# Attention and MoE block in one kernel: PSUM banks with fixed uses, 0.87 MoE steps a slot up to slot 108, chunk rows taken a slot later and loaded by one transfer

## The chip, the core and the metric

The kernel runs on one core of one Trainium2 chip. The core has a matrix engine (TensorE, PE in the profile, with its weight loads as PEld), a vector engine (VectorE, DVE), an activation engine (ScalarE, ACT), GpSimd (POOL) and an engine that here only issues transfers (SyncE, SP). Each works through its own instructions in order and waits for others by semaphores. Matmuls write into PSUM, which has 8 banks of 512 float32 columns in 128 partitions. The metric is the device time of one execution in microseconds (us); of several runs the median counts.

## The reference

Decay attention over 8 batches of 8 heads, 576 positions and head size 64, then a layer norm with a two-layer ReLU network on the 4608 tokens of width 512:

```python
scores = scale * np.matmul(q, k.transpose(0, 1, 3, 2))
cum = np.cumsum(np.log(np.clip(f, 0.0001, 1.0)), axis=-1)
decay = cum[:, :, :, None] - cum[:, :, None, :]
scores = np.where(causal, -1000000000.0, scores + decay)
attn = np.exp(scores - np.max(scores, axis=-1, keepdims=True))
attn = attn / (np.sum(attn, axis=-1, keepdims=True) + 1e-09)
x = np.matmul(attn, v)            # heads side by side: 8 x 576 x 512
...
xn = (x - mu) / np.sqrt(var + 1e-06) * g_ln
ch = np.maximum(xn @ w_ch1, 0.0) @ w_ch2     # 512 -> 2048 -> 512
return x + ch
```

## The kernel before

**Slots.** The attention of the 64 heads is cut into slots (line 1115): a head n has four, t = 1 to 4, one for each 128 rows of scores (the 64 rows of t = 0 go with t = 1). 7 more slots empty the pipeline. The loop of line 1132 goes through the slots u and calls, letter by letter, the pieces of an order string (lines 59 to 63; from slot 56 on the third). So the program order on every engine is written out by hand. The letters that matter here: Q scores of this slot's rows (qk_mm), S their row maxima on VectorE (softmax_a, line 411), e the exponential (ACT), B the normalising (POOL), t the transposition of a slot some slots back (transpose_unit, 2 slots back before head 14 and 4 from there on, when the rows first go through a transfer, move, letter D), h and l the high and low halves of the transposed parts (ACT line 522, VectorE line 527), A the product with v (av_unit, at t = 2 and 4), F and a its way out of PSUM (ACT line 606, VectorE line 617). From slot 56 on A, t and Q are dealt into one sequence (dealt). Matmuls are made of float32 halves, a high and a low one, so most products appear two or three times.

**MoE steps.** Between them runs the network over chunks of 256 tokens. One step is 1/16 of a chunk: M computes 128 hidden units of its tokens (mm1, lines 649 to 651, twelve matmuls into a bank h), r and m take their high and low half (ACT line 657, VectorE line 662), N adds the second layer of the step before into two accumulator banks acc0 and acc1 (mm2, lines 671 to 673, six matmuls). 14 chunks (224 steps) are made in this way, the last 1024 tokens by another scheme at the end, the wide part (wide_part). A slot has a step when can() says that the weights and the tokens are there (line 1153); R (rest) sets the limit of chunks whose attention is done, prefetches the next chunk's x (chunk_load, chunk_split, lines 633 and 634), and with 5 and 3 steps to go transposes the chunk's rows back (chunk_rows, line 694, rows loaded by rows_load two steps earlier, four transfers each). After a chunk's last mm2, chunk_out (line 731) takes the result from acc and stores it, within N.

**After the slots.** What is left of the 224 steps follows in the loop of line 1258, and with each of these steps one of five pieces of preparation for the wide part (wide_start): loads, differences (POOL line 903), splits (ACT line 915).

**PSUM.** Two banks are the accumulators. The other six are one ring: bank(name) gives the next of the six to whatever asks, be it scores (s), transposed parts (tr, tr_4b), products with v (o), hidden units (h) or rows (xp). A bank's next user waits for the readers of its last one.

**Numbers.** The steps before stand in slots 38 to 69, 74 to 105 and 107 to 262, and 4 of them after the slots.

Of the kernel before, what the change touches and what calls it, by code (L numbers as in the profile page):

```python
# [17 lines left out]
P = 128  # L18
KT = DM // P
# [12 lines left out]
LAG, LAG_MOVED = 2, 4  # L32
AV, AV_MOVED = 1, 3
MOVED = 14
PLAIN_CHUNKS = 14
WIDE = (NCHUNK - PLAIN_CHUNKS) // 2
PAIRS = FT // 2
EVEN_FROM = 1000
SUMS_FROM = 92
# [19 lines left out]
ORDERS = [  # L59
    (0, "WwbQsSthAeMrgFmlLNPaRf"),  # L60
    (37, "WwbQSstAMhPelgLNFrfmBRa"),
    (56, "WwAthQFlMSPNgreamLRDBZ"),
]
# [3 lines left out]
def attn_moe(ctx: ExitStack, tc: tile.TileContext, qk, v, f, g, w1, w2, out):  # L67
# [302 lines left out]
    def qk_mm(h, t):  # L370
        q0, m, w = QT[t]
        todo = []

        def mm(*a, **k):
            todo.append(lambda: nc.tensor.matmul(*a, **k))  # L375

        cuts = [(0, w)] if w <= 512 else [(0, w // 2), (w // 2, w)]
        h.s = getattr(h, "s", {})
        h.s[t] = []
        for i, (a, z) in enumerate(cuts):  # L380
            sp = bank(f"s{h.n}_{t}_{i}")[:m, : z - a]
            xq, kl = h.xq[:, q0 : q0 + m], h.kl[:, a:z]
            if h.plain:
                mm(sp, xq, kl, start=True, stop=True)
            else:
                mm(sp, h.hi[:, 0, q0 : q0 + m], h.hi[:, 1, a:z], start=True, stop=False)
                mm(sp, xq, kl, start=False, stop=True)
            h.s[t].append((a, z, sp))
        return todo
# [65 lines left out]
    def transpose_unit(h, t):  # L455
# [11 lines left out]
        if t <= 2:  # L467
            tp = bank(f"tr{n}_{t}")
            if t == 1:
                tr(tp[0:64, 0:128], rows_of(h, 0)[:, 0:D])  # L470
                tr(tp[0:64, 64:192], pt[:, 0:64])
                tr(tp[:, 192:320], pt[:, 64:192])
            else:
                tr(tp[0:64, 0:128], pt[:, 0:64])
                tr(tp[:, 128:256], pt[:, 64:192])
                tr(tp[:, 256:384], pt[:, 192:320])
            h.banks = [tp]
        else:
            tp = bank(f"tr{n}_{t}").rearrange("p (k c) -> p k c", k=4)
            tr(tp[0:64, 0, :], pt[:, 0:64])  # L480
            for k in range(1, 4):
                tr(tp[:, k, :], pt[:, 64 + P * (k - 1) : 64 + P * k])
            h.banks = [tp]
            if t == 4:
                tp = bank(f"tr{n}_4b")[:, :P]
                tr(tp, pt[:, 64 + 3 * P : 64 + 4 * P])
                h.banks.append(tp)
# [41 lines left out]
    def av_unit(h, t):  # L529
        po = bank(f"o{h.n}_{t}")  # L530
        todo = []
# [111 lines left out]
    def mm1(c):  # L643
        j = c.j
        c.j += 1
        fs = slice(P * j, P * j + P)
        ph = bank(f"h{c.n}_{j}")[:, :C]
        for k in range(KT):
# [26 lines left out]
    def tokens(c, k, t0, m, out_):  # L675

        t = t0
        while t < t0 + m:
            b, o = divmod(t, S)
            src, o0, lim = (xd1[b], 0, S1) if o < S1 else (xd2[b], S1, S)  # L680
            w = min(t0 + m - t, lim - o)
            nc.sync.dma_start(out=out_[:, t - t0 : t - t0 + w], in_=src[P * k : P * k + P, o - o0 : o - o0 + w])
            t += w

    def rows_load(c, i):
        c.xw = m2(f"xw{c.n}_{i}", F32).rearrange("p (k c) -> p k c", k=KT)
# [189 lines left out]
    class Wide:  # L876
# [122 lines left out]
    def wide_part():  # L999
        banks = [bank(f"wide{i}") for i in range(6)]  # L1000
        ba, bb, bc = [b[:, :C] for b in banks[:3]]
# [33 lines left out]
        for g in range(WIDE * PAIRS):  # L1035
# [96 lines left out]
    for u, slot in enumerate(slots):  # L1132
# [30 lines left out]
        def piece(c):  # L1163
# [149 lines left out]
```

## Time and profile before

| | |
|---|---|
| timed runs | 1200.33, 1201.69, 1202.26 us; median 1201.69 |
| profiled execution | 1199.95 us; span from first to last instruction 1198.1 us |
| mean granted TensorE clock | 0.990 |
| instructions | 26041 |
| TensorE waits, longest groups | tr for POOL 4.6 us (4 times), h for VectorE and ScalarE some 2 us |
| transfers | 246.46 MB, mean 206 GB/s, 64.8% of 16 engines' span |

In the rows that follow, a line such as L649 is the line of the kernel before. A row of the timeline gives start, duration, engine, line, operation, output<-input, shape, and in brackets the idle time of the engine before it with what ended it. A matmul's duration is longer than the distance to the next one, since matmuls are pipelined; what a matmul costs is read from the starts. A row of the stretches gives the stretch and its length, then the busy time of each engine with the number of its instructions, the granted clock, and the share and rate of the transfers.

### The profile page before, as it was taken

What the parts mean: (1) busy time and instruction counts of PE and PEld (TensorE: products, weight loads), DVE (VectorE), ACT (ScalarE), POOL (GpSimd) and SP (SyncE); (2) the same over time, 40 slices, a digit from 0 to 9 for tenths busy, and PEclk for the clock granted to TensorE, in tenths of its full rate; (3) what the DMA queues carried; (4) which work ended last, traced back from release to release, by engine and by line L of the source; (5) the groups of instructions that cost most, each with busy time, mean ns of one, the idle gap of its engine ahead of it and who ended that gap; (6) DMA issues with size and microseconds to landing.
All of it is one profiled execution on the core that took longest, in us unless ns stands there. A gap on an engine that the chain in (4) does not pass through costs nothing.

```text
span 1198.1 us, 26041 instructions
## 1 busy us (share of the span) xinstructions
PE 1174.0 (98%) x8044; PEld 1046.2 (87%) x8044; DVE 799.3 (67%) x2918; ACT 666.5 (56%) x1966; POOL 512.2 (43%) x621
## 2 busy tenths in 40 slices
PE   7998999989999999999999999999999999999998
PEld 5666889979999899999999999998999999899897
DVE  5787637676766768686768686867677774536443
ACT  5888655555656666556566665556565642323221
POOL 3668553434354555555445545455445431102000
PEclk8998999989999999999999999999999999999999
DMA  7788654666666776766876768686676664655542
GB/s 205 216 250 264 205 156 140 215 193 199 216 210 195 234 246 197 241 209 209 255 223 216 239 195 254 195 255 215 219 244 222 191 212 135 210 173 171 174 141 91
DMA packets 181914, 246.46 MB, mean 206 GB/s; under 512 B 39952, under 2 KB 113680, under 8 KB 181776
## 3 DMA queue, kind: packets, MB, share of 16 engines
q1 hardware_dynamic: 181776, 244.81, 64.8%
q8 instruction: 64, 1.05, 0.4%
q14 instruction: 74, 0.61, 0.2%
HBM read 163.76 MB, written 31.75 MB: 163 GB/s over the span
## 4 chain that ended last, share of the span: by engine, by line
PE 72%; DVE 3%; DMA 2%; issue 1%; SPq 1%; ACT 0%; POOL 0%; DVEq 0%; ACTq 0%; POOLq 0%
PE h L649 7%; PE h L650 7%; PE h L651 7%; PE acc L671 7%; PE acc L672 7%; PE acc L673 7%; PE s L375 6%; PE o L534 6%; PE tr L463 3%; PE wide L1011 2%; PE wide L1013 2%; PE wide L1012 2%; PE wacc L1026 1%; PE wide L1027 1%; PE wide L1026 1%; PE wacc L1027 1%
## 5 line engine op out<-in xcount | busy, mean ns | idle before, releaser
L429 POOL TENSOR_SCALAR p<-p,st 64x64 f32<-64x64 f32 (+4 forms) x320 | 173.3, 545 | 429.3 <-DVE st L428 90.5
L649 PE MATMUL h<-x,w1h 128*128 128x256 f32 x896 | 257.1, 287 | 2.1 <-DVE xs L617 1.0
L650 PE MATMUL h<-x,w1h 128*128 128x256 f32 x896 | 254.0, 283 | 0.9 <-DVE x L634 0.9
L651 PE MATMUL h<-x,w1l 128*128 128x256 f32 x896 | 253.2, 283 | 0.0
L422 ACT ACTIVATE p<-p,st 64x64 f32<-64x64 f32 (+4 forms) x320 | 178.3, 558 | 62.1 <-DVE st L411 54.1
L522 ACT CAST ph<-tr 64x128 fp32r<-64x128 f32 (+4 forms) x416 | 117.9, 332 | 113.9 <-PE tr L463 94.1
L671 PE MATMUL acc<-w2h,hh 128*128 128x512 f32 x448 | 176.3, 394 | 0.0
L672 PE MATMUL acc<-w2s,hh 128*128 128x512 f32 x448 | 176.1, 393 | 0.0
L649 PEld LDWEIGHTS h<-x,w1h 128*128 128x128 f32 x896 | 170.7, 191 | 5.9 <-DVE xs L617 2.0
L657 ACT ACTIVATE hh<-h 128x256 fp32r<-128x256 f32 x224 | 86.0, 384 | 161.0 <-PE h L651 159.1
L673 PE MATMUL acc<-w2h,hh 128*128 128x512 f32 x448 | 175.5, 392 | 0.0
L650 PEld LDWEIGHTS h<-x,w1h 128*128 128x128 f32 x896 | 170.8, 191 | 2.8 <-DVE x L634 1.7
L651 PEld LDWEIGHTS h<-x,w1l 128*128 128x128 f32 x896 | 170.6, 190 | 0.0
L411 DVE CUSTOM_DVE_ANT_0 p<-s,mask 64x64 f32<-64x64 f32 (+4 forms) x320 | 130.5, 420 | 17.1 <-PE s L375 5.6
L527 DVE TENSOR_TENSOR ph<-tr,ph 64x192 fp32r<-64x192 f32 x208 | 62.6, 301 | 103.2 <-ACT ph L522 99.4
L662 DVE SCALAR_TENSOR_TENSOR hh<-h,hh 128x256 fp32r<-128x256 f32 x224 | 94.2, 420 | 48.8 <-ACT hh L657 45.4
L375 PE MATMUL s<-hi 128*64 128x64 f32 x336 | 109.4, 333 | 2.4 <-DVE pl L527 1.4
L463 PE MATMUL tr<-identr,pq 128*128 128x128 f32 (+1 forms) x700 | 107.6, 227 | 1.4 <-DMA pq<-p 1.0
L673 PEld LDWEIGHTS acc<-w2h,hh 128*128 128x128 f32 x448 | 84.1, 188 | 18.8
L527 DVE TENSOR_TENSOR pl<-tr,ph 128x128 fp32r<-128x128 f32 x208 | 95.3, 458 | 3.8
L375 PE MATMUL s<-kl,xq 66*64 66x64 f32 x336 | 97.0, 293 | 0.0
L463 PEld LDWEIGHTS tr<-identr,pq 128*128 128x128 f32 (+1 forms) x700 | 82.0, 130 | 14.8 <-DVE st L411 0.7
(146 smaller groups left out, 2587.2 us busy)
## 6 DMA issues: line engine op xcount, KB each, us to landing
w2s<-w2d SPq DMA_DIRECT2D x224, 256.0 KB
raw<-in_qk_dram SPq DMA_DIRECT2D x56, 576.0 KB
wr<-in_w_dram SPq DMA_DIRECT2D x32, 512.0 KB
s<-sd SPq DMA_DIRECT2D x64, 256.0 KB
pq<-p SPq DMA_DIRECT2D x50, 288.0 KB
pq<-p SPq DMA_DIRECT2D x50, 224.0 KB
vr<-in_v_dram SPq DMA_DIRECT2D x64, 160.0 KB
wide<-w2d SPq DMA_DIRECT2D x32, 256.0 KB
```

The lines of the kernel that those rows point to most:

```text
L375: todo.append(lambda: nc.tensor.matmul(*a, **k))
L411: nc.vector.tensor_tensor_reduce(out=pt[:m, a:z], in0=sp, in1=mask[:m, off + a : off + z], scale=-SCALE, scalar=3.0e38 if i == 0 else st[: ...
L422: nc.scalar.activation(pt[:m, :w], pt[:m, :w], AF.Exp, bias=st[:m, i : i + 1], scale=-1.0, accum_out=st[:m, 2:3])
L429: nc.gpsimd.tensor_scalar(out=pt[:m, :w], in0=pt[:m, :w], scalar1=st[:m, 3:4], scalar2=1.0, op0=ALU.mult, op1=ALU.mult)
L463: todo.append(lambda: nc.tensor.transpose(out_.bitcast(F32R), in_, identr[:m, :m]))
L527: nc.vector.tensor_tensor(out=lo, in0=tp, in1=hi.bitcast(F32), op=ALU.subtract)
L649: mm(ph, w1h[:, k, fs], c.x[k][:, 0, :], start=(k == 0), stop=False)
L650: mm(ph, w1h[:, k, fs], c.x[k][:, 1, :], start=False, stop=False)
L651: mm(ph, w1l[:, k, fs], c.x[k][:, 0, :], start=False, stop=(k == KT - 1))
L671: mm(c.acc[i], h[:, 0, ts_], w2h[:, j, :], start=(j == 0), stop=False)
L672: mm(c.acc[i], h[:, 0, ts_], low, start=False, stop=False)
L673: mm(c.acc[i], h[:, 1, ts_], w2h[:, j, :], start=False, stop=(j == FT - 1))
```

## The change

Four parts.

1. From slot 60 on the six ring banks have fixed uses (class Fixed): bank 0 holds h, in two halves in turn; bank 1 holds o in columns 0 to 319 and the fifth transposition of t = 4 in columns 320 to 447; banks 2 and 3 hold scores in turn (t = 0 and t = 1 share one), banks 4 and 5 transposed parts and rows in turn. The wide part takes the same six in another order.
2. From slot 38 to slot 107 a credit grows by 0.87 a slot and a step takes 1 of it; from slot 108 it grows by the steps left over the slots left. Before, every slot that could have a step had one.
3. chunk_out is no longer called in N: a new letter O, first in every order, calls it in the next slot (store). In the loop after the slots it stands after the first layer, in the wide part after product p7.
4. The row loads take all four 128-wide parts in one transfer (tokens with a three-dimensional target), the wide part's loads two.

```diff
+FIXED_FROM = 60
-EVEN_FROM = 1000
+EVEN_FROM = 108
+EARLY_RATE = 0.87
 ORDERS = [
...
-    (56, "WwAthQFlMSPNgreamLRDBZ"),
+    (56, "OWwAthQFlMSPNgreamLRDBZ"),
...
+        def take(self, kind, name):
+            if not self.on:
+                return bank(name)
+            if kind in self.turns:
+                self.turns[kind] ^= 1
+            k = self.turns.get(kind)
+            b = self.banks
+            if kind == "h":
+                return b[0][:, 256 * k : 256 * k + 256]
+            if kind == "o":
+                return b[1][:, 0:320]
+            if kind == "t4":
+                return b[1][:, 320:448]
+            return b[2 + k] if kind == "s" else b[4 + k]
...
-            sp = bank(f"s{h.n}_{t}_{i}")[:m, : z - a]
+            if fixed.on and t < 2:
+                if t == 0:
+                    h.s_bank = fixed.take("s", "")
+                sp = h.s_bank[:m, 0:64] if t == 0 else h.s_bank[:m, 64:256]
+            else:
+                sp = fixed.take("s", f"s{h.n}_{t}_{i}")[:m, : z - a]
...
     def rows_load(c, i):
-        for k in range(KT):
-            tokens(c, k, c.n * C + P * i, P, c.xw[:, k, :])
+        tokens(c, 0, c.n * C + P * i, P, c.xw)
...
                 if j == FT - 1:
-                    chunk_out(c)
+                    self.out = c
                 self.prev = None
+
+        def store(self):
+
+            if self.out is not None:
+                chunk_out(self.out)
+                self.out = None
...
-        banks = [bank(f"wide{i}") for i in range(6)]
+        banks = [fixed.banks[i] for i in (2, 3, 4, 5, 0, 1)]
...
+        if u == FIXED_FROM:
+            fixed.start()
...
-        if u >= EVEN_FROM:
-            credit += moe.left() / (len(slots) - u)
+        if u >= FIRST_MOE + 3:
+            credit += EARLY_RATE if u < EVEN_FROM else moe.left() / (len(slots) - u)
             want = want and credit >= 1.0
             credit -= want
```

Three places show how instructions move. In the program after, lines are some 28 to 38 higher, and the names fixed_2770 to fixed_2775 are the banks 0 to 5.

On TensorE, from the scores of slot 71 (head 17, t = 4) on; hi and kl are halves of q and k. Before:

```order
L375 MATMUL s_4_0_3531<-hi_3118 128x288
L375 MATMUL s_4_0_3531<-kl_3119,xq_1294 128x288
L375 MATMUL s_4_1_3532<-hi_3118 128x288
L375 MATMUL s_4_1_3532<-kl_3119,xq_1294 128x288
L534 MATMUL o_2_3566<-ph_16_3364,vv_3506 128x320
L534 MATMUL o_2_3566<-ph_16_3364,vv_3506 128x256
```

and after:

```order
L403 MATMUL fixed_2772<-hi_2994 128x288
L403 MATMUL fixed_2772<-kl_2995,xq_1294 128x288
L403 MATMUL fixed_2773<-hi_2994 128x288
L403 MATMUL fixed_2773<-kl_2995,xq_1294 128x288
L682 MATMUL fixed_2770<-x_0_2132,w1h 128x256
L683 MATMUL fixed_2770<-x_0_2132,w1h 128x256
L684 MATMUL fixed_2770<-x_0_2132,w1l 128x256
```

Where the next slot's product with v followed at once, a step now stands between (its first three matmuls are shown).

On TensorE, the transpositions of head 16's fifth part in the same slot, with the semaphores that an instruction waits for. Before:

```order
L463 MATMUL tr_4_3529<-identr,pq_4_3415 128x128 [waits DMAHW4_49,PE_49]
L463 MATMUL tr_4_3529<-identr,pq_4_3415 128x128 x2
L463 MATMUL tr_4b<-identr,pq_4_3415 128x128
L463 MATMUL tr_4_3529<-identr,pq_4_3415 64x128
L375 MATMUL s_4_0_3531<-hi_3118 128x288
L375 MATMUL s_4_0_3531<-kl_3119,xq_1294 128x288
L375 MATMUL s_4_1_3532<-hi_3118 128x288 [waits DVE_49,PE_49]
```

and after:

```order
L496 MATMUL fixed_2775<-identr,pq_4_3223 128x128 [waits DMAHW0_49,Activation_49]
L496 MATMUL fixed_2775<-identr,pq_4_3223 128x128 x2
L496 MATMUL fixed_2771<-identr,pq_4_3223 128x128 [waits DVE_49]
L496 MATMUL fixed_2775<-identr,pq_4_3223 64x128
L403 MATMUL fixed_2772<-hi_2994 128x288
L403 MATMUL fixed_2772<-kl_2995,xq_1294 128x288
L403 MATMUL fixed_2773<-hi_2994 128x288
```

The wait for VectorE has moved from the scores to the fifth transposition, which goes to bank 1; what it waits for is the VectorE add that reads o in the slot before.

On VectorE, chunk_out of chunk 6 (xt<-acc). Before:

```order
L411 ISA p_4_8965,st_4_8966<-s_4_1_8936,mask,st_4_8966 128x288
L411 ISA st_4_8966 128x1
L731 SCALAR_TENSOR_TENSOR xt_0_8563<-acc_0_7988,rs_8566,xt_0_8563 128x512
L731 SCALAR_TENSOR_TENSOR xt_1_8713<-acc_1_7989,rs_8566,xt_1_8713 128x512
L662 SCALAR_TENSOR_TENSOR hh_0_8981<-h_0_8952,hh_0_8981 128x256
```

and after:

```order
L695 SCALAR_TENSOR_TENSOR hh_0_8685<-fixed_2770,hh_0_8685 128x256
L460 TENSOR_SCALAR st_0_8668<-st_0_8668 64x1
L461 RECIPROCAL st_0_8668<-st_0_8668 64x1
L460 TENSOR_SCALAR st_1_8671<-st_1_8671 128x1
L461 RECIPROCAL st_1_8671<-st_1_8671 128x1
L769 SCALAR_TENSOR_TENSOR xt_0_8310<-acc_0_7759,rs_8313,xt_0_8310 128x512
L769 SCALAR_TENSOR_TENSOR xt_1_8440<-acc_1_7760,rs_8313,xt_1_8440 128x512
L560 TENSOR_TENSOR ph_39_8647<-fixed_2774,ph_39_8647 64x128
```

The two operations stood ahead of the low half of the step's hidden units (L662) in slot 4 of a head; now they stand behind it (L695), at the start of a slot 2, ahead of the low halves of the transposed parts (L560).

More of the change, by code (lines that the diff above doesn't have):

```diff
@@ L59 @@
 ORDERS = [
-    (0, "WwbQsSthAeMrgFmlLNPaRf"),
-    (37, "WwbQSstAMhPelgLNFrfmBRa"),
-    (56, "WwAthQFlMSPNgreamLRDBZ"),
+    (0, "OWwbQsSthAeMrgFmlLNPaRf"),
+    (37, "OWwbQSstAMhPelgLNFrfmBRa"),
+    (56, "OWwAthQFlMSPNgreamLRDBZ"),
 ]
@@ L81, in bank, with __init__, start @@
         return ps.tile([P, 512], F32, tag="b", bufs=6, name=name)
+    class Fixed:
+        def __init__(self):
+            self.on, self.turns = False, {"h": 0, "s": 0, "tr": 0}
+        def start(self):
+            self.on, self.banks = True, [bank(f"fixed{i}") for i in range(6)]
+        def take(self, kind, name):
[12 more added lines that the diff above has]
+            return b[2 + k] if kind == "s" else b[4 + k]
+    fixed = Fixed()
     def m2(name, dt):
@@ L467, in transpose_unit @@
         if t <= 2:
-            tp = bank(f"tr{n}_{t}")
+            tp = fixed.take("tr", f"tr{n}_{t}")
             if t == 1:
@@ L478, in transpose_unit @@
         else:
-            tp = bank(f"tr{n}_{t}").rearrange("p (k c) -> p k c", k=4)
+            tp = fixed.take("tr", f"tr{n}_{t}").rearrange("p (k c) -> p k c", k=4)
             tr(tp[0:64, 0, :], pt[:, 0:64])
@@ L484, in transpose_unit @@
             if t == 4:
-                tp = bank(f"tr{n}_4b")[:, :P]
+                tp = fixed.take("t4", f"tr{n}_4b")[:, :P]
                 tr(tp, pt[:, 64 + 3 * P : 64 + 4 * P])
@@ L529, in av_unit @@
     def av_unit(h, t):
-        po = bank(f"o{h.n}_{t}")
+        po = fixed.take("o", f"o{h.n}_{t}")
         todo = []
@@ L646, in mm1 @@
         fs = slice(P * j, P * j + P)
-        ph = bank(f"h{c.n}_{j}")[:, :C]
+        ph = fixed.take("h", f"h{c.n}_{j}")[:, :C]
         for k in range(KT):
@@ L675, in tokens @@
     def tokens(c, k, t0, m, out_):
+        n = 1 if len(out_.shape) == 2 else out_.shape[1]
         t = t0
@@ L681, in tokens @@
             w = min(t0 + m - t, lim - o)
-            nc.sync.dma_start(out=out_[:, t - t0 : t - t0 + w], in_=src[P * k : P * k + P, o - o0 : o - o0 + w])
+            part = src[P * k : P * k + P * n, o - o0 : o - o0 + w]
+            cs = slice(t - t0, t - t0 + w)
+            if len(out_.shape) == 2:
+                nc.sync.dma_start(out=out_[:, cs], in_=part)
+            else:
+                nc.sync.dma_start(out=out_[:, :, cs], in_=part.rearrange("(k p) t -> p k t", p=P))
             t += w
@@ L686, in rows_load @@
         c.xw = m2(f"xw{c.n}_{i}", F32).rearrange("p (k c) -> p k c", k=KT)
-        for k in range(KT):
-            tokens(c, k, c.n * C + P * i, P, c.xw[:, k, :])
+        tokens(c, 0, c.n * C + P * i, P, c.xw)
     def chunk_rows(c, i):
-        tp = bank(f"xp{c.n}_{i}")
+        tp = fixed.take("tr", f"xp{c.n}_{i}")
         for k in range(KT):
@@ L735, in attn_moe @@
     class Moe:
-        cur, nxt, prev, step = None, None, None, None
+        cur, nxt, prev, step, out = None, None, None, None, None
         limit = 0
@@ L890, in load @@
             self.b[i, j] = b = self.tile(f"b{i}{j}_")
-            for k in range(2):
-                tokens(self, 2 * i + k, self.t0 + C * j, C, b[:, k, :])
+            tokens(self, 2 * i, self.t0 + C * j, C, b)
         def sum(self, i):
@@ L1076, in wide_part @@
             nc.gpsimd.tensor_tensor(out=c22, in0=u3, in1=s5, op=ALU.add)
+            moe.store()
             renew("p7")
@@ L1225, in piece @@
                 moe.second()
+            elif c == "O":
+                moe.store()
             elif c == "P":
@@ L1262, in attn_moe @@
             moe.first_low()
+        moe.store()
         run_later(RSTD)
```

## The prediction

> **What bounds the kernel now.** The page comes first, then the busy time by stretch, then the order of time around each stretch in which TensorE (PE) stood still.
>
> ```profile
> span 1198.1 us, 26041 instructions
> PE 1174.0 (98%) x8044; PEld 1046.2 (87%) x8044; DVE 799.3 (67%) x2918; ACT 666.5 (56%) x1966; POOL 512.2 (43%) x621
> PE 72%; DVE 3%; DMA 2%; issue 1%; SPq 1%; ACT 0%; POOL 0%; DVEq 0%; ACTq 0%; POOLq 0%
> ```
>
> PE is busy for 98% of the span and carries 72% of the chain that ended last; no other engine has more than 3% of it. The change adds and removes no matmul. So the time can only move by what PE loses: idle time, and time at half clock. The question is where the 24 us of idle lie and which of them the change reaches.
>
> ```profile
> core 0: us, PE busy (x) PEld busy (x) DVE busy (x) ACT busy (x) POOL busy (x), PEclk, DMA share, GB/s
> 454.10:477.20 23.10, 23.10 (x168) 21.37 (x167) 18.26 (x67) 14.00 (x42) 11.83 (x14) 1.00 0.59 195
> 454.10:465.24 11.14, 11.14 (x83) 10.25 (x81) 10.53 (x39) 7.43 (x24) 4.96 (x6) 1.00 0.39 129
> 402.40:979.30 576.90, 575.83 (x4201) 531.62 (x4199) 421.09 (x1604) 348.63 (x1053) 287.00 (x349) 1.00 0.71 223
> 252.40:273.60 21.20, 16.39 (x96) 13.60 (x95) 15.86 (x57) 12.53 (x38) 9.46 (x12) 0.84 0.61 198
> 392.20:402.40 10.20, 9.16 (x65) 8.01 (x63) 8.80 (x32) 6.80 (x21) 5.50 (x6) 1.00 0.80 248
> 1016.00:1030.00 14.00, 12.00 (x77) 10.54 (x76) 11.73 (x23) 5.99 (x13) 5.06 (x4) 1.00 0.92 297
> ```
>
> The first row is six undisturbed slots (3, 4, 1, 2, 3, 4 of a head, each with one MoE step), the second its first three. PE is never idle in them; slots 108 to 255 (third row) are the same, 1.07 us idle in 576.90. Here no other engine sets the pace. The losses are in the last three rows. The first of them, 252.40 to 273.60, holds slots 70 to 75, again 3, 4, 1, 2, 3, 4: the slots 70 to 73 have no step there, because chunk 2 may not start before slot 71. What is a step worth?
>
> ```profile
> 501.55 0.28 PE L649 MATMUL h<-x,w1h 128*128 128x256 f32 x1
> 502.98 0.40 PE L671 MATMUL acc<-w2h,hh 128*128 128x512 f32 x1
> 504.36 0.37 PE L463 MATMUL tr<-identr,pq 128*128 128x128 f32 x3
> ```
>
> By starts, its twelve first-layer matmuls hold PE for 1.43 us and its six second-layer ones for 1.38: 2.81. Six slots with two steps instead of six should take 23.10 - 4 x 2.81 = 11.86 us; they took 21.20. **9.3 us are lost there.** In the same way slots 106 to 108 (slot 106 has no step) should take 11.14 - 2.81 = 8.33 and took 10.20: **1.9 us**. At the start of the wide part 14.00 - 12.00 = **2.0 us**.
>
> ```profile
> 258.25 0.21 PE L375 MATMUL s<-hi 128*64 128x64 f32 x1 [1.05 <-DVE pl L527]
> 261.54 1.30 PE L534 MATMUL o<-ph,vv 128*128 128x256 f32 x5 [1.23 <-DVE st L411]
> ```
>
> Without steps PE waits for VectorE, whose latency 2.8 us of matmuls usually cover. And the clock falls:
>
> ```profile
> 103.29:106.71 3.42, 1.70 (x14) 1.51 (x15) 3.38 (x15) 2.77 (x7) 3.34 (x4) 1.00 0.69 183
> 106.71:113.53 6.82, 6.82 (x24) 4.62 (x23) 3.44 (x9) 5.28 (x16) 3.84 (x5) 0.50 0.86 287
> 256.89:260.31 3.42, 1.80 (x13) 1.27 (x13) 2.23 (x9) 0.88 (x3) 0.64 (x1) 1.00 0.83 295
> 260.31:267.13 6.82, 5.10 (x22) 4.58 (x22) 4.39 (x20) 5.18 (x17) 2.85 (x4) 0.50 0.81 262
> 393.43:396.84 3.41, 2.92 (x23) 2.54 (x21) 3.41 (x9) 2.35 (x7) 2.63 (x3) 1.00 0.65 185
> ```
>
> Twice a 3.42 us stretch with PE half busy (1.70, 1.80) is followed by 6.82 us at a granted 0.50; after one with 2.92 busy, the single gap of slot 106, the clock stays. The Trainium skill ("TensorE: Matmul & The Clock Gate", HAM oscillation) gives the rule as no idle gaps over about 3.4 us. The longest wait above is 1.23 us, so by that rule the clock would not have fallen at all; the trace decides, and half a stretch idle is enough. By the rule the first rival below would have no chance.
>
> **The rate.** Before: steps in slots 38 to 69 (32), 74 to 105 (32), 107 to 262 (156), and 4 after the slots. After: the credit grows by 0.87 a slot from slot 38, so the slots 38, 45, 53, 61, 68, 76, 84, 91, 99 and 107 have none; 60 steps stand in 39 to 106, one in every slot from 108 to 262 (155), 9 after the slots. When slot 71 opens chunk 2, chunk 1 still has steps, so the four-slot gap is gone, and slot 107's gap finds chunk 4 loaded.
> - Gain: 9.3 + 1.9, as far as the ten single gaps don't give it back.
> - Five steps move behind the slots: 5 x 2.81 = 14.05 us there, and as much less in slots 38 to 107 wherever PE sets the pace, thus nothing.
> - A single gap costs between nothing and what slot 106 cost.
>
> ```profile
> 396.87 0.38 PE L650 MATMUL h<-x,w1h 128*128 128x256 f32 x1 [0.52 <-DVE x L634]
> 398.07 0.28 PE L463 MATMUL tr<-identr,pq 128*64 128x128 f32 x2 [0.31 <-PE o L534]
> 399.26 0.39 PE L649 MATMUL h<-x,w1h 128*128 128x256 f32 x1 [0.20 <-DVE st L411]
> ```
>
> Its 0.52 us is the late split of the next chunk's x, which a gap inside a chunk doesn't have; 0.31 and 0.20 are h and tr waiting for a ring bank that o or s had. From slot 60 on no bank goes from one kind to another. Between 0 and 1.9 I take 0.3 for each of nine: +2.7.
> - The tenth, slot 38, lies where VectorE, not PE, is nearly full:
>
> ```profile
> 111.70:122.90 11.20, 10.45 (x62) 8.58 (x61) 10.13 (x32) 7.93 (x23) 7.83 (x8) 0.92 0.72 210
> 122.90:199.00 76.10, 76.10 (x501) 64.71 (x499) 45.74 (x171) 43.06 (x128) 35.32 (x39) 1.00 0.54 166
> ```
>
> VectorE is busy 10.13 of 11.20 us in slots 38 and 39, so a step taken away there may shorten nothing and still cost its 2.81 us later; at the other end it saves all of it. I take +1.0. The second row shows slots 40 to 55 PE-bound, so the gaps of 45 and 53 are like the others.
>
> **The steps behind the slots.** The wide part starts with this wait:
>
> ```profile
> 1011.79 1.30 POOL L903 TENSOR_TENSOR t<-b,b 128x512 f32<-128x512 f32 x1 [18.07 <-DMA b<-xa]
> 1021.14 0.36 PE L1011 MATMUL wide<-xp,s 128*128 128x256 f32 x1 [1.72 <-ACT xp L915]
> ```
>
> Loads, differences and splits of the wide operands are spread over four tail steps now. With nine, four of them (11.2 us) come after the last split was issued: -2.0, at worst 0.
>
> **Fixed banks, from slot 60.** The banks are followed as a whole: a write to one waits for the last reader of any part of it. h keeps both halves in bank 0, so each step's first matmul waits for VectorE's low half of the step before (L662); o and the fifth transposition (tr_4b) share bank 1, so tr_4b waits for VectorE's add of the o of the slot before (L617).
>
> ```profile
> 567.31 0.42 DVE L617 TENSOR_TENSOR xs<-o,ot 64x256 f32<-64x256 f32 x1
> 567.76 0.42 DVE L662 SCALAR_TENSOR_TENSOR hh<-h,hh 128x256 fp32r<-128x256 f32 x1
> 568.06 0.25 PE L463 MATMUL tr_4b<-identr,pq 128*128 128x128 f32 x1
> 568.80 0.28 PE L649 MATMUL h<-x,w1h 128*128 128x256 f32 x1
> 473.13 0.25 PE L463 MATMUL tr_4b<-identr,pq 128*128 128x128 f32 x1
> 473.28 0.42 DVE L617 TENSOR_TENSOR xs<-o,ot 64x256 f32<-64x256 f32 x1
> 852.47 0.25 PE L463 MATMUL tr_4b<-identr,pq 128*128 128x128 f32 x1
> 853.29 0.42 DVE L617 TENSOR_TENSOR xs<-o,ot 64x256 f32<-64x256 f32 x1
> 821.61 0.39 PE L649 MATMUL h<-x,w1h 128*128 128x256 f32 x1 [0.31 <-DVE xs L617]
> 522.55 0.39 PE L650 MATMUL h<-x,w1h 128*128 128x256 f32 x1 [0.34 <-DVE x L634]
> ```
>
> In the usual head the add ends at 567.73, 0.33 us before tr_4b starts, and the low half at 568.18, 0.62 before h: no wait. But at 473 the add ends 0.57 us after tr_4b, at 852 1.24 after. Seven of the 36 heads of slots 108 to 255 are late so, by 4.7 us in sum; with some 0.06 us of signal each (h at 821.61 followed an add that ended at 821.55) that is 5.1 us of new waits. Behind tr_4b stand the scores and the step, so PE loses all of it. Against it, two late heads already cost PE a wait of h for the same add (821.61, and one like it at 853.76), about 0.5 us each; two of the seven stand ahead of a chunk's first step, where the square-root steps and splits now fall into other slots (0.8); two waits for x (522.55 and one more) cost about 0.9. I take 5.1 - 1.0 - 0.8 - 0.9 = +2.4; the ends are +5.1 and -2.9 (no late add, and all those waits gone).
>
> **Rows out and rows in.** The two operations that take a chunk from the accumulators (L731) leave the slot's middle, where they stand ahead of L617 and L662, for the start of the next:
>
> ```profile
> L731 DVE SCALAR_TENSOR_TENSOR xt<-acc,rs,xt 128x512 f32<-128x512 f32 x28 | 19.7, 745 | 1.1 <-PE acc L673 1.0
> 467.78 0.42 DVE L662 SCALAR_TENSOR_TENSOR hh<-h,hh 128x256 fp32r<-128x256 f32 x1
> 470.10 0.29 PE L649 MATMUL h<-x,w1h 128*128 128x256 f32 x1
> ```
>
> 1.5 us a chunk; behind them now stand the low halves of the transposed parts, the row maxima and the low half of h. From slot 112 on they fall into a head's slot 2, where (last two rows) the low half of h ends at 468.20, 1.9 us before the next h: hidden. Left in the middle of a slot, ahead of L662, they would make h wait in its new way. The next chunk's first second-layer matmul waits for them too; that slot's transpositions, scores and a first layer of 1.43 us lie between. The row loads shrink from four transfers to one, the same bytes, used two steps later; the wide loads from two to one: nothing. Should the one transfer land later, the gap of two slots (7.8 us) is its cover.
>
> **Sum.** -9.3 - 1.9 - 2.0 + 2.7 + 1.0 + 2.4 = -7.1 us. The profiled execution took 1199.95 us (span 1198.1), the median of the three timed runs is 1201.69, 1.74 above it. From the profile 1192.9, as a median **1194.6**.
>
> **Rivals.**
> - The clock falls once more after slot 38 (12%). PE has little work there: half a stretch idle was enough at 103.29. Against it: of the 10.45 us that PE was busy in slots 38 and 39, 7.6 remain without the step, two thirds of the stretch. Price: half of 6.82 us, 3.4: 1198.0.
> - The single gaps don't pay (10%): each costs what slots 106 to 108 lost apart from the late split, 1.9 - 0.7 = 1.2, so 9 x 1.2 = 10.8 instead of 2.7: 1202.7, no change.
> - The shared bank 1 (10%), **slower**. If the add is late as at 473 (0.57 + 0.06) in every head of slots 60 to 255, 48 x 0.63 = 30.2 us replace the 2.4: 1222. It decides from a mean wait of 0.25 us a head, 12 us in all: 1204.2. The Trainium skill ("PSUM — Partial Sum Buffer", Summary: rules for kernel authors) asks for a different bank, or for a semaphore by bank, where PSUM is read while a matmul runs; the order of the instructions shows just such a wait at tr_4b. What speaks against it is the usual 0.33 us of slack.
> - The costs don't come (15%): gaps, slot 38 and banks at 0, -13.2: 1188.5.
> - That the gap stays although the rate is changed: the steps' order excludes it, except as a wait for x at chunk 2, which the rivals above cover.
>
> **How the numbers follow.** The forecast has 53%, and 1190 to 1199 as its own range. Out of 1188.5 to 1202.5 stay the shared bank, part of the case without costs and of the gaps that don't pay, about 2 in 10. About 0.2% (2.4 us) is what a measurement can tell from no change. Faster by more: the forecast, the case without costs and most of the clock's case, 0.76; within: the gaps that don't pay, a part of the clock's and of the mildest bank case, 0.15; slower: 0.09.
>
> **What will show it.** No 0.50 clock after 120 us and no six slots over 22 us near slot 70; PE at the wide start without the 1.72 us; tr_4b's bank with waits for the add in about one head in five. It is wrong if PE's idle time rises between slots 108 and 255 by more than 7 us, if a third stretch at 0.50 stands after slot 38, or if the slots with a gap are as long as those with a step.

## The result: slower where faster was forecast

| | before | after |
|---|---|---|
| median of the timed runs | 1201.01 us (4 runs, 1199.40 to 1202.26) | 1207.92 us (4 runs, 1207.31 to 1208.89) |
| ratio after / before | | 1.0059, 95% interval 1.0042 to 1.0076 |
| profiled execution: time, span | 1199.95, 1198.1 us | 1207.31, 1205.5 us |
| mean granted TensorE clock | 0.990 | 0.994 |

The kernel is 0.6% slower, by more than its measurement is uncertain; 1194.6 us had been predicted. The page of the changed kernel has these lines for those shown of before, and two of its costliest groups (the number behind the second bar is the idle time of the engine ahead of the group, then what ended most of it):

```profile
span 1205.5 us, 25882 instructions
PE 1174.4 (97%) x8044; PEld 1043.4 (87%) x8044; DVE 798.1 (66%) x2918; ACT 665.3 (55%) x1966; POOL 511.7 (42%) x621
L496 PE MATMUL fixed<-identr,pq 128*128 128x128 f32 (+1 forms) x750 | 110.0, 229 | 6.6 <-DVE xs L650 5.7
L683 PEld LDWEIGHTS fixed<-x,w1h 128*128 128x128 f32 x820 | 155.8, 190 | 3.8 <-DVE x L667 2.7
```

PE does the same work and loses more time. The first group is the transpositions; tr_4b among them waits 5.7 us for the add of o, as the prediction feared. The second is the first layer, whose weight loads wait for the low half of x (L667); the prediction knew two such waits in the kernel before, and counted them as gone.

Where the time went is seen when both traces are cut at the same slots. A slot begins with its first score matmul; the rows are slots 0 to 37, 38 to 59, 60 to 75, 76 to 107, 108 to 254, and the rest. Before, then after:

```profile
9.86:111.74 101.88, 94.84 (x479) 62.43 (x480) 73.19 (x294) 81.38 (x244) 63.69 (x77) 0.93 0.81 241
111.74:213.74 102.00, 101.25 (x662) 86.77 (x661) 64.25 (x235) 58.75 (x173) 48.62 (x53) 0.99 0.57 173
213.74:273.62 59.88, 55.07 (x380) 49.38 (x379) 42.40 (x169) 35.08 (x107) 25.34 (x32) 0.94 0.62 199
273.62:398.22 124.60, 123.56 (x906) 114.12 (x904) 88.75 (x347) 74.86 (x229) 56.60 (x71) 1.00 0.64 207
398.22:979.26 581.04, 579.76 (x4227) 535.08 (x4226) 424.30 (x1618) 351.67 (x1061) 288.62 (x351) 1.00 0.71 224
979.26:1198.10 218.84, 212.60 (x1368) 191.67 (x1366) 101.74 (x251) 60.00 (x150) 25.30 (x28) 1.00 0.50 159
```

```profile
9.86:107.93 98.07, 92.89 (x479) 61.51 (x480) 72.87 (x293) 80.51 (x240) 63.23 (x77) 0.95 0.82 242
107.93:208.13 100.20, 95.39 (x610) 79.75 (x608) 64.86 (x233) 59.13 (x173) 49.25 (x54) 0.98 0.57 177
208.13:265.21 57.08, 56.75 (x417) 52.13 (x415) 42.19 (x169) 35.23 (x108) 25.43 (x32) 1.00 0.65 205
265.21:384.57 119.36, 114.39 (x836) 104.17 (x834) 85.33 (x329) 72.67 (x222) 57.25 (x71) 1.00 0.68 215
384.57:974.04 589.47, 582.51 (x4227) 536.00 (x4225) 423.41 (x1623) 351.29 (x1062) 287.88 (x351) 1.00 0.69 219
974.04:1205.52 231.48, 226.75 (x1458) 204.31 (x1456) 104.84 (x268) 62.09 (x157) 25.20 (x28) 1.00 0.49 158
```

The number of PE's instructions shows which steps moved. To compare lengths, the moved work (1.43 us for a first layer, 1.38 for a second) is taken out: three steps less in slots 38 to 59 (8.43 us), two more in 60 to 75 (5.62), five first and four second layers missing instead of one and one in 76 to 107 (9.86), one second layer less behind slot 108 (1.38), five steps more at the end (14.05). What is left is lost or won time, and stands here beside the prediction's terms:

| slots | difference | less the moved work | predicted | its terms |
|---|---|---|---|---|
| 0 to 37 | -3.8 | -3.8 | 0 | |
| 38 to 59 | -1.8 | **+6.6** | +1.6 | slot 38, gaps 45 and 53 |
| 60 to 75 | -2.8 | -8.4 | -8.7 | four-slot gap -9.3, gaps 61 and 68 |
| 76 to 107 | -5.2 | **+4.6** | -0.4 | slot 106 -1.9, five gaps |
| 108 to 254 | +8.4 | **+9.8** | +2.4 | banks |
| the rest | +12.6 | -1.4 | -2.0 | start of the wide part |
| sum | +7.4 | +7.4 | -7.1 | |

The gain came as forecast (60 to 75). Three stretches cost more: the gaps before slot 60, those after 76, and, most of all, the long even stretch behind slot 108. The first row lies within what executions differ by (last section).

### The profile page after: what moved, and what is told of

Its sections match the earlier page's. It is cut to its first block, busy times and chain, and to the rows that moved or that the text cites. A ratio compares the mean times of both kernels' runs of the same rounds, so it can differ in the third digit from the quotient of the medians.

```text
span 1205.5 us, 25882 instructions
## 1 busy us (share of the span) xinstructions
PE 1174.4 (97%) x8044; PEld 1043.4 (87%) x8044; DVE 798.1 (66%) x2918; ACT 665.3 (55%) x1966; POOL 511.7 (42%) x621
## 4 chain that ended last, share of the span: by engine, by line
PE 59%; DVE 7%; DMA 2%; issue 1%; ACT 1%; SPq 0%; DVEq 0%; POOL 0%; ACTq 0%
PE fixed L683 6%; PE fixed L682 6%; PE fixed L684 6%; PE acc L705 5%; PE acc L704 5%; PE acc L706 5%; PE fixed L403 5%; PE fixed L567 4%; PE fixed L496 3%; PE fixed L1054 2%; PE fixed L1056 2%; PE fixed L1055 2%; DVE p L444 1%; PE wacc L1069 1%; PE fixed L1069 1%
## 5 line engine op out<-in xcount | busy, mean ns | idle before, releaser
L682 PE MATMUL fixed<-x,w1h 128*128 128x256 f32 x820 | 234.7, 286 | 3.9 <-DVE hh L695 2.8
L683 PE MATMUL fixed<-x,w1h 128*128 128x256 f32 x820 | 232.4, 283 | 0.7
L684 PE MATMUL fixed<-x,w1l 128*128 128x256 f32 x820 | 231.5, 282 | 0.0
L555 ACT CAST ph<-fixed 64x128 fp32r<-64x128 f32 (+4 forms) x450 | 121.4, 325 | 89.6 <-PE fixed L496 87.6
L682 PEld LDWEIGHTS fixed<-x,w1h 128*128 128x128 f32 x820 | 155.7, 190 | 7.9 <-DVE hh L695 4.4
L683 PEld LDWEIGHTS fixed<-x,w1h 128*128 128x128 f32 x820 | 155.8, 190 | 3.8 <-DVE x L667 2.7
L684 PEld LDWEIGHTS fixed<-x,w1l 128*128 128x128 f32 x820 | 155.8, 190 | 0.0
L560 DVE TENSOR_TENSOR ph<-fixed,ph 64x192 fp32r<-64x192 f32 x200 | 60.2, 301 | 90.6 <-ACT ph L555 87.0
L496 PE MATMUL fixed<-identr,pq 128*128 128x128 f32 (+1 forms) x750 | 110.0, 229 | 6.6 <-DVE xs L650 5.7
L695 DVE SCALAR_TENSOR_TENSOR hh<-fixed,hh 128x256 fp32r<-128x256 f32 x205 | 86.1, 420 | 29.8 <-ACT hh L690 26.7
L560 DVE TENSOR_TENSOR pl<-fixed,ph 128x128 fp32r<-128x128 f32 (+2 forms) x250 | 101.5, 422 | 3.6
L444 DVE CUSTOM_DVE_ANT_0 p<-fixed,mask 64x64 f32<-64x64 f32 (+4 forms) x245 | 99.3, 419 | 0.7 <-DMA pq<-p 0.7
L403 PE MATMUL fixed<-hi 128*128 128x288 f32 (+4 forms) x294 | 95.5, 330 | 0.0
```

Source lines behind the costliest of these rows:

```text
L496: todo.append(lambda: nc.tensor.transpose(out_.bitcast(F32R), in_, identr[:m, :m]))
L555: nc.scalar.copy(out=hi, in_=tp)
L560: nc.vector.tensor_tensor(out=lo, in0=tp, in1=hi.bitcast(F32), op=ALU.subtract)
L682: mm(ph, w1h[:, k, fs], c.x[k][:, 0, :], start=(k == 0), stop=False)
L683: mm(ph, w1h[:, k, fs], c.x[k][:, 1, :], start=False, stop=False)
L684: mm(ph, w1l[:, k, fs], c.x[k][:, 0, :], start=False, stop=(k == KT - 1))
```

## The experiments

### Taking the change apart

Four kernels: the rate alone; the change without the rate; the change with tr_4b elsewhere; the change without the fixed banks.

```diff
 # e1: the kernel before, with the condition and the credit of the change
-        if u >= EVEN_FROM:
-            credit += moe.left() / (len(slots) - u)
+        if u >= FIRST_MOE + 3:
+            credit += EARLY_RATE if u < EVEN_FROM else moe.left() / (len(slots) - u)
 # e2: the changed kernel with these lines as before and EVEN_FROM = 1000
 # e3: the changed kernel
-            if kind == "t4":
-                return b[1][:, 320:448]
+            if kind == "t4":
+                kind = "tr"
 # e4: the changed kernel (and the wide part's banks from the ring)
-        if u == FIXED_FROM:
-            fixed.start()
```

> The kernel before with the new step rate alone (0.87 a slot up to slot 108, even from there); banks, rows out and rows in as before. Gap theory: in the trace of the changed kernel PE waits for VectorE around nearly every slot without a step between 76 and 108 (about 1.2 us each at slots 76, 91, 99, 107) and in slots 38 to 60 (4.8 us idle), so the rate pays back what the four-slot gap cost and the five steps behind the slots weigh on top: within 3 us of the kernel before (1198 to 1204), with idle PE ahead of h in slots 93 and 101. Bank theory: the loss is the fixed banks alone; then the rate gives what was predicted for it, -9.3 - 1.9 - 2.0 + 2.7 + 1.0 = -9.5 us, about 1191.5, and slots 93 and 101 have no wait ahead of h.

> The changed kernel with the old step rate (no step in slots 70 to 73 and 106, four steps behind the slots); fixed banks, rows out and rows in as changed. Bank theory: from slot 60 on tr_4b waits for the add of the o before it, 5.0 us of idle in slots 108 to 255 and some 1.5 before, with 1.5 to 3 us of waits of h for the low half: 7 to 10 us slower than the kernel before, 1208 to 1211. Gap theory alone (the rate did all of it): within 2 us of the kernel before, 1199 to 1203.

> The changed kernel with one line other: tr_4b takes the next bank of the two that the transpositions use by turns, not the rest of the bank of o. No wait of tr_4b for the add is possible any more. Bank theory (shared bank 1): the excess of PE ahead of tr_4b, 8.1 us from slot 60 on by matmul starts (6.7 of it behind slot 108), goes: 1199 to 1201. Rival: the add is late because VectorE is late, and PE then waits for VectorE one instruction further on (the o or the h behind it): less than 3 us gained, 1205 to 1208.

> The changed kernel with the ring of six banks instead of the fixed ones; rate, rows out and rows in as changed. Bank theory: as fast as with tr_4b apart and the waits of h for the low half (2.8 us) gone too, 1197 to 1200. Gap theory alone: no gain, 1206 to 1208. Either way this run less the one with the new rate alone gives rows out and rows in together, which were put at nothing: a difference of at most 1 us.

The ratios of the tables are to the kernel before as it ran in the same series: 1199.03 us here, 1200.26 and 1201.62 in the next two tables, 1201.01 for the changed kernel. The slots of the last column are those of a head, 1 to 4.

| kernel | median us | ratio to before (95%) | slots 108 to 254 | chunks start in slot |
|---|---|---|---|---|
| before, run beside them | 1199.03 | 1 | 581.04 | 4 |
| changed | 1207.92 | 1.0059 | 589.47 | 1 |
| e1 rate alone | 1213.86 | 1.0121 (1.0107 to 1.0135) | 589.80 | 1 |
| e2 without the rate | 1206.93 | 1.0069 (1.0053 to 1.0085) | 586.50 | 4 |
| e3 tr_4b apart | 1215.60 | 1.0141 (1.0127 to 1.0154) | 596.50 | 1 |
| e4 ring | 1204.95 | 1.0051 (1.0036 to 1.0067) | 590.03 | 1 |

Most of the expectations missed. The rate alone is slower than the whole change, outside what either theory gave. Taking tr_4b out of bank 1 made the kernel slower, not faster: now the transpositions follow each other differently in banks 4 and 5 and wait for ACT's copy of the rows (xt), 5.4 us, beside 2.2 us of h and a fall of the clock at 577 us. And without any fixed bank the stretch behind slot 108 loses as much as with them. The groups of that stretch, of the changed kernel and of e4 (last: idle time, and all that ended it):

```profile
L682 PE MATMUL fixed<-x,w1h 128*128 128x256 f32 x588 | 168.1, 286 | 0.6 <-DVE hh L695 0.6
L496 PE MATMUL fixed<-identr,pq 128*128 128x128 f32 (+1 forms) x555 | 82.1, 230 | 5.7 <-DVE xs L650 5.0 <-DVE pl L560 0.7
```

```profile
L682 PE MATMUL h<-x,w1h 128*128 128x256 f32 x588 | 168.8, 287 | 3.1 <-ACT x L666 2.1 <-DVE xs L650 0.3 <-DVE st L444 0.2
L496 PE MATMUL tr<-identr,pq 128*128 128x128 f32 (+1 forms) x518 | 80.4, 228 | 0.1
```

In e4 the 5.0 us of tr_4b are gone, and h waits 2.1 us for x instead. The last column of the table gave the new theory, that of the phase: the slot of a head in which chunks begin. Every kernel with the new rate has its chunks begin in a head's slot 1, since ten slots without a step, in place of five, shift the first step of chunk 4 from slot 107 (t = 4) to 112 (t = 1); from there on one step follows in each slot, and 16 steps are four heads, so all later chunks begin there too. The last two of a chunk's four pieces of x are split only when the old chunk's last step has been issued (fetch: room is 2 until then), so the first step waits on ACT and VectorE. The timeline of the changed kernel in slot 160, a first slot (starting at 594.14; selected rows of ACT, VectorE, PE and PEld):

```profile
594.55 0.78 ACT L455 ACTIVATE p<-p,st 128x576 f32<-128x576 f32 x1 [1.75 <-DVE st L444]
594.85 0.39 PE L682 MATMUL fixed<-x,w1h 128*128 128x256 f32 x1
595.32 0.70 ACT L666 CAST x<-xr 128x256 fp32r<-128x256 f32 x2
595.74 0.76 DVE L667 TENSOR_TENSOR x<-xr,x 128x256 fp32r<-128x256 f32 x2 [0.68 <-ACT x L666]
596.22 0.19 PEld L683 LDWEIGHTS fixed<-x,w1h 128*128 128x128 f32 x1 [0.27 <-DVE x L667]
```

The exponential of slot 159's 576 columns stands ahead of the splits on ACT. They end 2.36 us into the slot; the step, begun 0.71 us into it, wants its third piece after six matmuls, about 1.4 us into it. Slot 160 takes 4.34 us here, 4.85 in e4 and, with no chunk start, 3.58 before.

So it is for all of them. From first score to first score, the nine first slots between 112 and 240 take 4.65 us on average in e4, where the other slots with t = 1 take 3.58: 9.6 us in sum, nearly the whole loss of its stretch. In the changed kernel they take 4.13, 5.0 us in sum. The other half of its loss stands one slot earlier: of the nine waits of tr_4b behind slot 108 (5.0 us), seven lie ahead of the scores of the last slot before a chunk's start. Whether these waits are what makes the first slots behind them shorter than e4's, no run shows.

### Moving the chunk starts

Five, six and seven single gaps with the ring, and five with the fixed banks, all with rows out and rows in as changed:

```diff
-            credit += EARLY_RATE if u < EVEN_FROM else moe.left() / (len(slots) - u)
-            want = want and credit >= 1.0
-            credit -= want
+        want = want and u not in GAPS
 # e5 to e7 also: no fixed.start(), and the wide part's banks from the ring
 # e5, e8: GAPS = (61, 65, 69, 73, 89)
 # e6:     GAPS = (61, 65, 69, 73, 81, 97)
 # e7:     GAPS = (61, 65, 69, 73, 81, 89, 97)
```

> The changed kernel with the ring of six banks, and with five single slots without a step (61, 65, 69, 73, 89) instead of the rate of 0.87: so no step moves behind the slots, no gap lies in slots 38 to 60, and chunks 4 to 13 start again in a head's slot 4 (the changed kernel: slot 1). Phase theory: the stretch of slots 108 to 255 loses time in every kernel in which chunks start in slot 1 (8.8 us in the one with the rate alone, 8.9 with rate, rows out and rows in), by 1.1 us in each chunk's first slot, where h waits for the softmax and for x. Here it comes back to the 581.0 us of the kernel before, within 1 us, and with the four-slot gap gone (-9.3) the whole is 0.991 of the kernel before, about 1190. Rival: what the stretch loses comes from rows out in the next slot or from the row loads; then it keeps 7 us or more and the whole is 0.997 or above.

> As the one with five gaps, but with six (61, 65, 69, 73, 81, 97), so that chunks 4 to 13 start in a head's slot 1; five steps behind the slots instead of four. Phase theory: 9 chunk starts of 1.1 us in slots 108 to 255, some 10 us more than with five gaps, 0.999 to 1.001 of the kernel before. Rival (the phase does nothing): one more gap, between nothing and 1.2 us: 0.991 to 0.993.

> As the one with five gaps, but with seven (61, 65, 69, 73, 81, 89, 97), so that chunks 4 to 13 start in a head's slot 2; six steps behind the slots. If slot 1 is dear because two softmaxes stand in it, slot 2 costs no more than slot 4 and two gaps more cost 0 to 2.4 us: 0.991 to 0.994 of the kernel before. If only slot 4 is cheap, 108 to 255 loses about 10 us as with six gaps: 0.999 or above.

> The changed kernel, fixed banks and all, with the five single gaps (61, 65, 69, 73, 89) instead of the rate. Phase theory with the banks: chunks start in slot 4, where the kernel with the old rate and the fixed banks lost 5.5 us between 108 and 255, 0.5 us of idle PE for h in each chunk; so 5 to 8 us above the same gaps with the ring, 0.995 to 0.998 of the kernel before. Bank theory in its first form (shared bank 1 costs 6.7 us behind slot 108 wherever the chunks start): tr_4b waits as in the changed kernel, 5 us of idle. Banks free: 0.991.

| kernel | chunks start in slot | median us | ratio (95%) | slots 108 to 254 |
|---|---|---|---|---|
| e5 ring, five gaps | 4 | 1194.31 | 0.9952 (0.9935 to 0.9969) | 580.88 |
| e6 ring, six | 1 | 1202.15 | 1.0018 (1.0007 to 1.0028) | 589.26 |
| e7 ring, seven | 2 | 1193.41 | 0.9936 (0.9923 to 0.9950) | 579.29 |
| e8 fixed banks, five | 4 | 1204.83 | 1.0030 (1.0017 to 1.0043) | 586.68 |

One gap more than five costs 8.4 us behind slot 108, and a further one takes 10.0 us off again. So it is not the number of gaps; it is the slot in which chunks begin. In e6 the ten first slots take 4.74 us on average where others with t = 1 take 3.58; in e7, with t = 2, 4.43 beside 4.39. Other work of a chunk (its rows, its way out) moves along with its start, and no run moves the splits alone; that they are what costs is read from these slots. The shared bank is no constant price either: with starts in slot 4 (e8) the transpositions wait 0.1 us behind slot 108, but h then waits 4.5 us for VectorE. e8 missed its 0.995 to 0.998, and e5 its 0.991, ahead of slot 108. The gap at 73 stands right ahead of chunk 2; the wait ahead of the scores of slot 75 in e5's timeline, and the three 3.41 us windows around it:

```profile
263.43 0.37 PE L402 MATMUL s<-hi 128*128 128x288 f32 x1 [1.68 <-DVE pl L559]
258.02:261.44 3.42, 3.18 (x22) 2.50 (x20) 1.73 (x7) 2.28 (x8) 1.35 (x2) 1.00 0.81 227
261.44:264.85 3.41, 1.55 (x11) 1.01 (x10) 3.37 (x10) 1.36 (x5) 2.14 (x3) 1.00 0.93 290
264.85:268.26 3.41, 3.41 (x15) 3.22 (x15) 2.61 (x11) 1.34 (x4) 1.09 (x2) 0.50 0.77 217
```

PE is busy 1.55 of 3.41 us, and the next window runs at half clock: the four-slot gap's loss in small. e8 has the same fall, and one wait of tr_4b of 2.99 us there.

### The changed kernel with starts in slot 2, and the parts that were put at nothing

```diff
 # e9: the changed kernel, MORE = 105
-            want = want and credit >= 1.0
-            credit -= want
+            want = want and credit >= 1.0 and u != MORE
+            credit -= want or u == MORE
 # e10: the ring, GAPS = (45, 49, 61, 65, 69, 81, 97), rows out and in as changed
 # e11: the kernel before with the same GAPS
 # e12: e11, with tokens as changed, and in rows_load (and alike in the wide part's load)
-        for k in range(KT):
-            tokens(c, k, c.n * C + P * i, P, c.xw[:, k, :])
+        tokens(c, 0, c.n * C + P * i, P, c.xw)
```

> The changed kernel with one more slot without a step (105), so that chunks 4 to 13 start in a head's slot 2 instead of 1, and ten steps behind the slots instead of nine; fixed banks and the rate stay. Phase theory: the 8.5 us that slots 108 to 255 lost against the kernel before go down to 1 or 2, against at most 1.3 us for one more gap: 6 to 8 us faster than the changed kernel, 0.998 to 1.001 of the kernel before. Bank theory: tr_4b's waits (5 us) stay wherever the chunks start, and the one gap more costs: 1.005 to 1.007.

> The ring with seven single gaps and chunks that start in slot 2, but with the gaps at 45, 49, 61, 65, 69, 81 and 97: none stands right ahead of the first step of chunk 2 (with the gap at 73 slots 74 and 75 took 11.0 us instead of 7.6, the clock at half in them). If that gap's place is the cost: 4 to 7 us less than with 73, 0.988 to 0.990 of the kernel before. If a gap before slot 60 costs what the three of the new rate cost there on average (1.3 us each), and chunk 2 is late anyway: 0.993.

> The kernel before with the seven gaps 45, 49, 61, 65, 69, 81, 97 and nothing else of the change: rows out in the middle of the slot, rows in by four transfers, the ring. Prediction: rows out and rows in are worth nothing, so within 1 us of the same gaps with both. Rival: the kernel with the rate alone was 0.7% (8.4 us) above the one with rate, rows out and rows in; if that is rows out or in, it comes back here: 0.995 to 0.997 of the kernel before.

> As the one before it, with the rows (and the wide part's) loaded by one transfer; rows out stays in the middle of the slot. If four transfers in a row hold up the transposed weights on the DMA queues (two waits of PE for pq, 2.2 and 0.9 us, and one of 2.2 us for a second-layer weight stood in the kernel with the rate alone, none in that with one transfer), this is as fast as with rows out in the next slot too. If rows out is what matters, it is as slow as with the old rows.

| kernel | median us | ratio (95%) | slots 108 to 254 |
|---|---|---|---|
| e9 changed, one gap more | 1201.16 | 1.0002 (0.9989 to 1.0016) | 580.21 |
| e10 ring, rows out and in changed | 1187.77 | 0.9886 (0.9871 to 0.9900) | 579.60 |
| e11 ring, old rows | 1197.55 | 0.9969 (0.9955 to 0.9982) | 584.37 |
| e12 ring, one transfer, rows out as before | **1186.15** | **0.9870** (0.9854 to 0.9885) | 577.96 |

e9 came out as the phase theory said: with one gap more, the changed kernel is level with the one before. Its splits end early, 0.87 us into slot 161, a first slot that starts at 594.35:

```profile
594.02 0.70 ACT L667 CAST x<-xr 128x256 fp32r<-128x256 f32 x2
594.45 0.76 DVE L668 TENSOR_TENSOR x<-xr,x 128x256 fp32r<-128x256 f32 x2 [0.18 <-ACT x L667]
594.71 0.28 PE L683 MATMUL fixed<-x,w1h 128*128 128x256 f32 x1
```

e10 against e7 shows the gaps' places: 45 and 49 in place of 73 and 89, thus none right ahead of chunk 2; slots 70 to 75 take 23.0 us, one step more in them, instead of 25.9. e10 to e12 separate the rows. Rows out in the next slot is worth nothing that can be told (the intervals of e10 and e12 overlap). e11, expected within 1 us of e10, came out as its rival said (0.995 to 0.997). One transfer for the rows, and two for the wide part's, are worth 1.0% here (0.9969 to 0.9870, intervals far apart). The row loads of e11, then of e12, grouped (count: shortest/median/longest issue in ns):

```profile
L682 SPq DMA_DIRECT2D xw<-xa x76: 378/430/1542, 154.1 to 999.3; - x76
L682 SPq DMA_DIRECT2D xw<-xb x60: 382/430/642, 225.7 to 992.8; - x60
```

```profile
L688 SPq DMA_DIRECT2D xw<-xa x19: 371/444/587, 153.1 to 986.6; - x19
L688 SPq DMA_DIRECT2D xw<-xb x15: 384/447/945, 224.5 to 980.1; - x15
```

The median issue holds SP's queue for 0.43 us in e11 and for 0.44 in e12, where it moves four times as much. 136 issues are 34 now, 45 us less on the queue that also issues the transposed weights (pq) and the second layer's (w2s). In e11 that queue works for 26 us, from 864.5 us on, without a pause of 0.25 us; in e12 the longest such stretch is 14 us. What stands in it comes late. The weight that slot 233 (from 881.95 us) wants for its second layer, its issue and PE's wait, in e11:

```profile
880.83 0.64 SPq L765 DMA_DIRECT2D w2s<-w2d  x1
882.27 1.81 SPq L682 DMA_DIRECT2D xw<-xa  x4
884.38 0.50 PE L672 MATMUL acc<-w2s,hh 128*128 128x512 f32 x1 [0.25 <-DMA w2s<-w2d]
885.13 0.47 SPq L444 DMA_DIRECT2D pq<-p  x1
887.42 0.25 PE L463 MATMUL tr<-identr,pq 128*64 128x128 f32 x1 [0.31 <-DMA pq<-p]
```

and the same weight and row load in e12, where slot 233 begins at 873.00 us:

```profile
869.19 0.63 SPq L770 DMA_DIRECT2D w2s<-w2d  x1
870.63 0.45 SPq L688 DMA_DIRECT2D xw<-xa  x1
```

3.8 us ahead of the slot instead of 1.1. The Trainium skill ("DMA: Bandwidth & Descriptors", Rules for kernel authors) advises to merge many small transfers into a large one. The runs agree, by 1.0%. The bytes are the same (246.5 MB) and the packets nearly so (181915 and 180089), so the issuing queue is the likely cause; all 6.4 us that e12 wins behind slot 108 stand in the slots with numbers 8 to 13 modulo 16, during and behind the row loads (5 to 9). No run relieves the queue in another way. In e12 PE is never idle behind slot 108, and the clock does not fall after 26 us:

```profile
382.25:960.21 577.96, 577.96 (x4229) 534.10 (x4227) 416.14 (x1628) 351.01 (x1063) 288.05 (x351) 1.00 0.71 225
```

## Why the prediction was wrong, step by step

- **The four-slot gap: right.** -8.4 measured where -9.3 + 0.6 was put; no half clock after it. e4's 56.16 us in these slots are what 59.88 - 9.34 + 5.62 gives.
- **"The square-root steps and splits now fall into other slots (0.8)" and the two waits for x, counted as gone (0.9): the step that failed.** The prediction saw that the chunk starts move and booked it as a gain of 1.7 us. They moved to slot 1, where the splits come too late: the nine first slots cost 5.0 us in the changed kernel and 9.6 with the ring. e6 against e5 and e7 (8.4 and 10.0 us) and e9 against the changed kernel (9.3 us) show what the slot of the starts is worth. It makes the difference between slower and level (e9: 1.0002); that the kernel is not faster lies with the gaps and the banks below.
- **The shared bank 1: the waits right, the price not.** 5.1 us of new waits were put and 5.0 came, in 9 heads of 36; with the 5.0 us of the late splits they are about the 9.8 us of the stretch. But they are no price of the bank alone: with starts in slot 2 (e9) 1.7 us of them are left, and in e4 they are gone and the first slots take as much more. What the fixed banks cost behind slot 108 depends on the phase: nothing with starts in slot 1 (589.47 against 590.03), 2.3 us with slot 2 (e9's 580.21 + 1.38 against e7's 579.29), 5.8 with slot 4 (e8 against e5). The 2.4 us of the prediction, put for slot 1, are near the value of slot 2 by chance. (Its lower end adds up to -2.7, not -2.9.) No run separates the bank of h from that of o, so how the price divides between them is open.
- **The single gaps: mis-sized, 2.7 + 1.0 put.** Before slot 60 three gaps lost 6.6 us. Slot 38 saved nothing, 2.8 us, the far end of its bound (without the step PE waits 1.36 us there, for POOL's p and not for VectorE, and in the kernel before not at all); slot 45 saved all; after 53, slot 55 grew from 4.53 to 6.69 us. The remaining 1.7 us are about what the rival's clock takes: half clock came at 121 us, for 3.41 us rather than 6.82 (last row below), and e4, which lacks it, passes slot 40 in 6.34 us instead of 7.84. From 76 to 107 the five gaps lost 6.5 us (4.6 net of slot 106's 1.9), in e4 3.7. Two waits of the changed kernel there, and the two clock windows:

```profile
267.32 0.47 PE L704 MATMUL acc<-w2h,hh 128*128 128x512 f32 x1 [1.39 <-DVE xt L769]
358.28 0.39 PE L682 MATMUL fixed<-x,w1h 128*128 128x256 f32 x1 [1.09 <-DVE st L460]
117.91:121.33 3.42, 2.59 (x13) 1.50 (x14) 3.27 (x10) 2.14 (x8) 2.15 (x3) 1.00 1.01 317
121.33:124.75 3.42, 3.42 (x16) 3.09 (x15) 1.11 (x8) 2.22 (x8) 0.75 (x1) 0.50 0.43 169
```

- **Rows out: "hidden" but once.** The first row above (1.45 us in e4) is slot 76, a gap one slot behind a chunk's start: the "first layer of 1.43 us" that was to lie between is missing there. The second row, slot 101, is the price of h in one bank. Slot 100 has no second layer after the gap of 99 and is 1.4 us shorter, so VectorE's low half of its h ends only at 358.22, and the next h, in the same bank, waits. With the ring there is no wait.
- **Rows in: "nothing" was wrong**, in the other direction. Bytes were counted, not the issues on SP. The rate alone (e1, 1.0121) against the rate with both row changes (e4, 1.0051) points the same way, though in other slots: 5.9 us of it lie between 76 and 107, where PE waits 2.2 us for pq in e1, and none behind 108. Without the one transfer the changed kernel would by this have been slower still. At the phase of the kernel before it is not seen behind slot 108: e5, with one transfer, takes 580.88 us where that kernel takes 581.04.
- **The moved steps: right at the end, wrong ahead.** +12.6 us came with the wide part's wait gone (14.05 - 1.4); "as much less in slots 38 to 107" did not, by what the gaps lost.
- **The signs.** PE's idle time behind slot 108 rose by 5.7 us (7.0 against 1.3), less than the 7 that were to show failure; the rest of the 9.8 lies in the starts around each wait, which idle time doesn't count (slot 160 is 0.76 us longer with 0.08 us idle in its step). "No 0.50 clock after 120 us" failed, at 121 us. "No six slots over 22 us" could not be met: six slots with a step each take 23.1 us undisturbed, and slots 70 to 75 took 23.8.

Of the rivals, the shared bank's is the only one that reaches the measured time (1204.2 to 1222), but not by its mechanism: the add was to be late in every head and was in 9 of 36, and without the shared bank (e3, e4) the stretch is no shorter. The gaps that don't pay (1202.7) had a real share: 6.6 and 6.5 us were lost there. None had the phase.

## What to carry to other kernels

Removing or adding one unit of work in a periodic schedule shifts the phase of all that follows: look which slot the rare events (a chunk's start) land in, and what stands ahead of their producers there; the same gap count plus one can be worth 8 us. Place single gaps by the slot, not by an average rate: 45, 49, 61 and 81 saved their whole step, while 38, 53 and, right ahead of a chunk's start, 73 lost 2 to 6 us. The slot of the head alone doesn't tell them apart, since all of these but 38 have t = 2. Count transfers as issues on their queue as well as bytes.

## What the hardware showed besides

The clock followed PE's busy share in windows of 3.41 us. In the 14 profiles, between 30 and 1150 us, 13 windows at full clock had PE busy for less than 54%, and 12 of them were followed by 0.50; of 27 with 54 to 64%, 3 were; of 73 with 64 to 80%, 4 were, all beginning between 117 and 121 us; of 4448 fuller ones none. So between 54 and 80% the share alone doesn't decide. No idle stretch of a whole window was needed: PE was busy for 37% or more in every window that half clock followed.

The same instructions up to slot 38 took 98.1 us in the changed kernel's profile and 102.5 in e8's, whose code differs from slot 38 on only, with the granted clock at 0.95 and 0.91:

```profile
9.86:112.35 102.49, 96.50 (x480) 64.03 (x480) 72.99 (x294) 81.55 (x244) 63.56 (x77) 0.91 0.81 240
```

The windows fall differently on the work from one execution to the next: within a profile all changes of the clock lie on one grid of 3.41 us, and its offset from the first instruction goes from 0.62 to 3.13 us over the 14 profiles. The Trainium skill ("TensorE: Matmul & The Clock Gate", Part 1) says that the window is free-running and does not reset with the kernel, and this agrees. So the -3.8 us of the first stretch lie within what executions differ by, and single profiles compare to within 4.4 us there.
